# Retiming the start of a fused attention and phase-mixing kernel: another engine for one root, an earlier table load, open theta sums, a last store on two queues

## The chip, the cores and the metric

The kernel runs on one core of one Trainium2 chip. The metric is the device time of one execution in microseconds, as the median of several runs. The core has five engines with an instruction queue each, and each queue is worked off in order: TensorE (PE, with PEld for its weight loads), VectorE (DVE), ScalarE (ACT), GpSimd (POOL) and SyncE (SP, which here issues nearly all DMA transfers). An instruction that waits holds up everything behind it in its own queue.

## The reference, cut to what matters

There are 8 batches of 576 tokens, 8 heads of 64, so 512 channels.

```python
kv  = einsum('bhsd,bhse->bhde', k, v)          # 64x64 for each head
out = einsum('bhsd,bhde->bhse', q, kv)
x   = out / sqrt(mean(out*out) + 1e-6) * g_norm # normed over each head's 64
theta = x @ w_theta
zr, zi = x*cos(theta), x*sin(theta)
y = einsum('ts,bsd->btd', w_tok_r, zr) + einsum('ts,bsd->btd', w_tok_i, zi)
u = x + y
result = u + maximum(u @ w_ch, 0)
```

## The kernel before, in words

A batch is cut into four blocks of 128 tokens and a tail, block 4, of 64 tokens. For each batch, with the line of the main instruction: the loads of q, k and v for the four head pairs (L415, L421); a cast of q to 16 bits (`qcast`, L600; the tail of q, `ql`, L606); turning q on PE (`qTps` L783, copied to `qT` L794/L796); k transposed times v on PE (`kv` L662), copied into a block-diagonal `kvbd` (L816/L818); the product `raw` (L823 by head pair, L699 by block); its square (`sq` L830/L706), the sum over 64 (`ss` L836/L710), one over the root (`rt`), the normed `xp` or `x` (L860/L733); its turn (`xTps` L871/L943, copied to `xT` L882/L884/L952); the phase `th` (L996, block 4 L1001), rounding (`pt` L1008 on ACT, `f` L1012 and `fa` L1019 on DVE), sine and cosine (`tr` L1031, block 4 L1039, on ACT), the product `z` (L1049); the token mix `y` (L1092), `uT` (L1103); the channel product `vps` (L1150), `u` turned back by PE (`ups` L1141, copied on ACT L1157) or by a transposing DMA (`ub`), the sum `ot` (L1161) and the store (L1168, block 4 in two halves L1173).

Batches 0 and 1 go by head pair (`by_pair`, L803), so that work starts when the first pair has landed; the others go by block. The root is taken in two ways. The head pairs of batch 0 and the tail block of batch 0 use ACT's Sqrt (L843, L725) and a reciprocal on DVE (L847, L729). All others use POOL: an addition (L851/L717) and a power of -0.5 (L855/L721). ACT's Sqrt and Sin come from different function tables. Sqrt's is loaded at the start, and the task `sin` (L563) loads Sin's once, after the last Sqrt.

The token-mix weights come by casting DMAs that POOL issues (`wnat`, `wnatl`, L511, L516), are turned on PE (`wTps` L579) and copied to `wT` (L587/L589). `w_theta` comes through a staging tile `wst` in four chunks and is cast to `wth` (L490 on ACT, L492 on DVE). `wch` (L544) is issued by POOL after the load of a given v tile (`WCH_AFTER`, by a small copy to `late`, L385).

The order on every engine is not written by hand. Every piece of work is a task with the engines that may do it, a cost, a due time, and the tasks and buffer slots it needs (`weave.add`). A list scheduler (`Weave.run`) goes through a modelled time and picks by start and due time; `DUE`, `PERIOD`, `START`, `SLOTS` and a few margins are its only knobs. Where PE would be idle the plan puts `warm` matmuls on a constant (L395) that nothing reads. Each engine gets its instructions in the order in which they were picked. Tiles have few buffers: `ql` has one, so that the load of batch 1's `ql` waits for the cast of batch 0's, with every later load behind it on SP's queue.

```python
BANK = {"th": "mm", "y": "mm", "vp": "mm", "pu": "tp", "px": "tp"}
SLOTS: "raw": 2, "tp": 2, "mm": 3, "k": 6, "v": 6, "q": 6, "ql": 1, ...
pu_on = not U_FROM <= b < B - 1 or ti == NF     # u by PE, else by DMA
```

Of the kernel before, what the change touches and what calls it, by code (L numbers as in the profile page):

```python
# [17 lines left out]

PERIOD = 26.95
START = 4.0  # L20
DUE = {
    "load": (-21.61, 8.44),
    "theta": (0.39, 0),
    "mixers": (17.6, 0),
    "wch": (24.7, 1.25),
    "wT": (21.7, 1.67),
    ("phase", 0): (19.67, 0),
    ("mix", 0): (28.68, 4.96),
    ("channel", 0): (31.53, 7.53),
    ("phase", 1): (11.06, 3.64),  # L30
    ("mix", 1): (31.68, 5.24),
    ("channel", 1): (50.99, 7.88),
    ("first", 1): (-24.56, 1.26),
    "first": (0.46, 0),
    "cast": (27.66, 0.92),
    "turn_q": (-15.49, 0.49),
    "attention": (-2.51, 1.53),
    "norm": (-1.15, 4.11),
    "turn": (4.17, 1.73),
    "phase": (18.31, 3.76),  # L40
    "mix": (51.46, 2.87),
    "channel": (75.2, 4.3),
}
# [8 lines left out]
Q_DMA = 4  # L52
U_FROM = 2
X_FROM = 8
MIX_AFTER = 2
WCH_AFTER = 8
KV_RUN = 1
Q_SOFT = 0
QL_SOFT = 1


class Transfers:

    LANES = 8

    def __init__(self):
        self.soft, self.hard, self.done = [], [], {}

    def serve(self, at, left):
        for (a, b) in self.soft:
            if at < a:
                step = min(a - at, left)
                (at, left) = (at + step, left - step)
            if left > 0 and at < b:
                step = min((b - at) / 2, left)
                (at, left) = (at + 2 * step, left - step)
        return at + left
# [4 lines left out]
    def add(self, name, at, took, soft):  # L84
        if soft:
            begin = max(at, self.soft[-1][1] if self.soft else 0.0)
            self.soft.append((begin, begin + 2 * took))
            self.done[name] = begin + 2 * took + 0.3
            free = None
            for (n, arrive, length) in self.hard[-24:]:  # L90
                if self.done[n] > begin + 0.2:
                    if free is None:
                        free = self.before[n]
                    self.before[n] = free
                    free = self.serve(max(arrive, free), length)
                    self.done[n] = free + 0.2
            return
        last = self.done[self.hard[-1][0]] - 0.2 if self.hard else 0.0
        if not self.hard:
            self.before = {}  # L100
        self.before[name] = last
        self.hard.append((name, at, took))
        self.done[name] = self.serve(max(at, last), took) + 0.2


class Weave:
# [7 lines left out]

    SLACK = {"PE": 0.2, "ACT": 0.004, "DVE": 0.078, "POOL": 0.1, "SP": 0.05}
    MARGIN = {"PE": 0.247, "ACT": 0.026, "DVE": 0.555, "POOL": 0.1, "SP": 0.0}
    BEGIN = {"PE": 1.6, "ACT": 3.2, "DVE": 1.7, "POOL": 2.5, "SP": 0.73}
    WARM = 69.7
    COLD = 5.0
    URGENT = 5.5  # L120
    AHEAD = 0.3
    HOLD = 2.45
    DRAIN = 0.095
# [21 lines left out]
    def run(self):  # L145
# [25 lines left out]
        while ready:  # L171
            best = {}
            for t in ready:
# [8 lines left out]
                for (e, cost, lat, port) in engines:  # L182
                    new = e == "PE" and self.ARRAY[port] != form
                    clear = free[e] + self.DRAIN if new else free[e]
                    start = max(clear, at + self.MARGIN[e], port_free if port is True else 0.0)
                    if name[0] == "warm" and start > self.WARM:
                        continue
                    if due < self.URGENT:
                        start = max(clear, start - self.AHEAD)
# [25 lines left out]
            if e == "PE" and not hot:  # L215
                if start > free[e] + 0.4:
                    streak = start
# [45 lines left out]
def kernel(  # L263
# [13 lines left out]
    nc = tc.nc  # L277
# [95 lines left out]
    def sp(cost):  # L373
        return ("SP", cost, cost, False)
# [4 lines left out]
    def soft(took):  # L379
        return (2.4, took, True)  # L380
# [21 lines left out]
    def load(b, hp):  # L402
# [48 lines left out]
        if hp == (0 if b else HP - 1):  # L451
            for (i, (kind, src)) in enumerate((("kl", k), ("vl", v), ("ql", q))):
                if b < QUAD and kind != "ql":
                    continue
                if kind == "ql" and QL_SOFT and b > 1:
                    def fetch(e):
# [4 lines left out]
                              needs=[("qc", b, 0)], uses=[f"qc{b}"], dma=soft(0.9))  # L461
                    continue
                weave.add((kind, b), [sp(0.64)], due("load", b, hp) + (0.04 if b else 1.15) + 0.01 * i,
                          tail(kind, src),
# [5 lines left out]
    def load_weights():  # L470
# [38 lines left out]
        for (i, w) in enumerate((moe_w_tok_r, moe_w_tok_i)):  # L509
# [8 lines left out]
            def part(which, i=i):  # L518
                def fn(e):
# [8 lines left out]
                    else:  # L528
# [5 lines left out]
            weave.add(("wnatl", i), [("POOL", 0.56, 0.56, False)], use + 0.2 + i, rest,  # L534
                      needs=["hold_mix"], dma=soft(0.5))
            weave.add(("wtt", i, 0), [act(P * 2), dve(0.3, True), pool(P * 2)], use + 8, part(0),
# [25 lines left out]
        def table(e):  # L562
            nc.scalar.activation(out=warm[:], in_=pio2_t[:], func=AFT.Sin)  # L563
        weave.add("sin", [("ACT", 1.5, 1.6, False)], due("first", 0, HP + 2), table,
                  needs=[("rt0", hp) for hp in range(HP + 1)] + [("xTp", 0, HP - 1)])

# [124 lines left out]
    def norm(b, ti):  # L691
# [30 lines left out]

        def root0(e):
            t = st[ss]
            nc.scalar.activation(out=t[:], in_=t[:], func=AFT.Sqrt, bias=eps_t[:])  # L725

        def invert0(e):
            r = st[rt] = sb("rt", [P, H], FP32, rt)
            nc.vector.reciprocal(r[:], st[ss][:])  # L729

        def scale(e):
# [27 lines left out]
        weave.add((ss,), [dve(0.59)], at, total, needs=[(sq,)], makes=[("ss", ss)], uses=[sq])  # L759
        if b == 0:  # L760
            weave.add(("rt0", HP), [("ACT", 0.2, 0.35, False)], at, root0, needs=[(ss,)], uses=[ss])
            weave.add((rt,), [dve(0.12)], at, invert0, needs=[("rt0", HP)], makes=[("rt", rt)],
                      uses=[ss])
        else:
            weave.add((rt,), [("POOL", 2.0, 2.1, False)], at, root, needs=[(ss,)], makes=[("rt", rt)],
                      uses=[ss])
        weave.add((x,), [dve(0.6)], at, scale, needs=[(rt,)], makes=[("x", x)], uses=[raw, rt])
# [35 lines left out]
    def by_pair(b, hp):  # L803
# [3 lines left out]
        home = "xT" if b else "uT"  # L807
        bank = "mm" if b == 0 and hp > 1 else "raw"
        (qTn, bdn, kvn, xn, xTn) = (f"{n}{b}" for n in ("qT", "bd", "kv", "xp", "xT"))
# [176 lines left out]
    def phase(b, ti):  # L986
# [58 lines left out]
        def apply(e):  # L1045
# [8 lines left out]
        full = ti < NF  # L1054
        weave.add((th,), [pe(0.866) if full else pe(0.436, "H")], at, product,
                  needs=([("xTp", b, hp) for hp in range(HP)] if b < 2 and full else [("xT", b, ti)])
                  + [("wth", kc) for kc in range(NK)],
                  makes=[(BANK["th"], th)], uses=[f"xT{b}"])
        weave.add((pt,), [act(n, 1)], at, whole, needs=[(th,)], makes=[("pt", pt)], uses=[th])
# [65 lines left out]
    def channel(b, ti):  # L1125
# [39 lines left out]
        def store(e):  # L1165
# [6 lines left out]
            for (half, r) in parts:  # L1172
                nc.sync.dma_start(out=out[b, SF:S, r * n:(r + 1) * n], in_=t[half])  # L1173

# [15 lines left out]
        elif ti == 0:  # L1190
            for kc in range(NK):
# [9 lines left out]
                  makes=[("ot", ot)], uses=[vp, u if pu_on else f"ub{b}"])  # L1201
        weave.add(("out", b, ti), [sp(0.46 if full else 0.9)], at, store, needs=[(ot,)],
                  uses=[ot], dma=dma(0.66 if full else 0.6))
# [64 lines left out]
```

## Time and profile before

| what | value |
|---|---|
| median of 6 runs | 214.2 us (213.51 to 216.27) |
| the profiled execution: time, span | 214.86 us, 213.1 us |
| PE busy | 203.7 us, 96% of the span, 2305 matmuls |
| DVE, ACT, POOL busy | 177.2, 150.3, 89.0 us |
| DMA moved | 45.62 MB, mean 214 GB/s |
| warm matmuls | 50 |
| granted PE clock | 0.99 |

The profile is one execution. The span runs from the first instruction to the last; about 1.8 us of the execution's time lie outside it. A row of the timeline gives the start, the length, the engine, the line and the tile. The length of one matmul or one DVE or ACT instruction contains its run-through time; what an engine needs for one in a row of them is the distance from start to start, which is shorter (0.216 us for a 512-wide matmul, 0.056 us for a 128-wide transpose, 0.60 us for a DVE instruction whose row says 0.69).

### The profile page before, as it was taken

The numbers are of one execution on the slowest core, as the hardware profiler recorded it, in microseconds if no ns is written. First come the engines' busy times: TensorE is split into PE (matmuls) and PEld (weight loads), VectorE is DVE, ScalarE is ACT, GpSimd is POOL, SyncE is SP. The second block draws the span as 40 slices with busy tenths as digits, with TensorE's granted clock in tenths as the row PEclk, the third lists the DMA queues.
The fourth block names the chain that finished last, engine by engine and source line by source line (L and its number), as shares of the span: only waits on it lengthen the run. The fifth ranks groups of instructions, "written<-read, shape, count | busy, mean of one in ns | idle before, by whom it ended". The sixth has DMA issues, their size and how long they took to land.

```text
span 213.1 us, 5833 instructions
## 1 busy us (share of the span) xinstructions
PE 203.7 (96%) x2305; PEld 144.5 (68%) x2305; DVE 177.2 (83%) x355; ACT 150.3 (71%) x294; POOL 89.0 (42%) x104
## 2 busy tenths in 40 slices
PE   6898989999999999999999999999999999999992
PEld 4775567876588777677777577765787467568560
DVE  3297589877978889999999998999999989973652
ACT  2166799967984999898897859789688588550031
POOL 8040106595106663474474436584475733000000
PEclk9996999999999999999999999999999999999999
DMA  6999999998587898978888999759874262334424
GB/s 179 389 365 253 266 366 284 378 236 173 105 273 240 214 287 291 242 261 175 243 175 152 297 345 204 146 142 284 254 166 86 88 174 63 140 109 98 145 104 172
DMA packets 62463, 45.62 MB, mean 214 GB/s; under 512 B 33380, under 2 KB 55524, under 8 KB 62436
## 3 DMA queue, kind: packets, MB, share of 16 engines
q1 hardware_dynamic: 58272, 43.01, 70.0%
q0 software_dynamic: 4160, 2.25, 8.3%
q8 instruction: 18, 0.29, 0.6%
q14 instruction: 9, 0.07, 0.1%
q10 hardware_dynamic: 4, 0.00, 0.0%
HBM read 33.06 MB, written 9.44 MB: 199 GB/s over the span
## 4 chain that ended last, share of the span: by engine, by line
PE 74%; ACT 10%; DMA 6%; DVE 6%; POOL 1%; issue 1%; SPq 1%; DVEq 0%
PE y L1092 29%; PE vps L1150 14%; PE th L996 11%; PE kv L662 7%; DMA wst<-in_moe_w_theta_dram 3%; PE xTps L943 3%; PE raw L699 3%; DMA k<-in_k_dram 2%; ACT tr L1031 2%; PE ups L1141 2%; PE warm L395 2%; PE th L1001 1%; ACT tr L1039 1%; ACT pt L1008 1%; DVE x L733 1%
## 5 line engine op out<-in xcount | busy, mean ns | idle before, releaser
L1092 PE MATMUL y<-wT,z 128*128 128x320 f16 (+1 forms) x576 | 78.1, 286 | 0.1
L1092 PEld LDWEIGHTS <-z 128*128 128x128 f16 x576 | 55.0, 98 | 16.2 <-issue 0.6
L721 POOL TENSOR_TENSOR rt<-ss,mhalf 128x8 f32<-128x8 f32 x31 | 55.8, 1801 | 2.6
L1150 PE MATMUL vps<-wch,uT 128*128 128x512 f16 (+1 forms) x192 | 36.3, 344 | 0.1
L1103 DVE SCALAR_TENSOR_TENSOR uT<-y,gcol,xT 128x320 f16<-128x320 f32 (+1 forms) x48 | 29.2, 610 | 6.9 <-PE y L1092 6.9
L1008 ACT ACTIVATE pt<-th,magic_t 128x512 f32<-128x512 f32 (+1 forms) x40 | 25.8, 645 | 9.2 <-PE th L996 5.8
L996 PE MATMUL th<-wth,xT 128*128 128x512 f16 x128 | 32.0, 379 | 0.0
L717 POOL TENSOR_SCALAR ss<-ss 128x8 f32<-128x8 f32 x31 | 8.4, 272 | 55.7 <-DVE ss L710 54.9
L1012 DVE SCALAR_TENSOR_TENSOR f<-pt,th 128x512 f32<-128x512 f32 (+1 forms) x40 | 25.0, 625 | 2.9 <-ACT pt L1008 2.9
L662 PE MATMUL kv<-v,k 128*64 128x64 f32 (+1 forms) x672 | 26.0, 226 | 0.4 <-DMA v<-in_v_dram 0.4
L662 PEld LDWEIGHTS kv<-v,k 128*64 128x64 f32 (+1 forms) x672 | 23.2, 140 | 4.2 <-issue 3.2
L1031 ACT ACTIVATE tr<-fa,pio_t 128x512 f16<-128x512 f32 x32 | 23.1, 721 | 1.8 <-DVE fa L1019 1.6
L1031 ACT ACTIVATE tr<-f 128x512 f16<-128x512 f32 x32 | 20.2, 631 | 5.5 <-DVE f L1012 5.3
L952 ACT ACTIVATE xT<-xTps,gcol 128x512 f16<-128x512 f16 (+1 forms) x32 | 20.1, 629 | 5.3 <-PE xTps L943 5.1
L710 DVE TENSOR_REDUCE ss<-sq 128x8 f32<-128x512 f32 x32 | 21.7, 678 | 2.2 <-ACT sq L706 2.2
L733 DVE TENSOR_TENSOR x<-raw,rt 128x512 f16<-128x512 f32 x32 | 21.9, 683 | 1.8 <-POOL rt L721 1.3
L1150 PEld LDWEIGHTS <-uT 128*128 128x128 f16 (+1 forms) x192 | 14.7, 102 | 11.4 <-issue 0.6
L1157 ACT COPY u<-ups 128x512 f16<-128x512 f16 (+1 forms) x20 | 9.9, 500 | 16.8 <-PE ups L1141 16.8
L1049 DVE TENSOR_TENSOR z<-x,tr 128x1024 f16<-128x1024 f16 (+1 forms) x32 | 19.6, 615 | 1.5 <-ACT tr L1039 1.2
L706 ACT ACTIVATE sq<-raw 128x512 f32<-128x512 f32 x32 | 19.0, 593 | 0.5 <-PE raw L699 0.5
L996 PEld LDWEIGHTS <-xT 128*128 128x128 f16 x128 | 11.5, 98 | 10.1 <-ACT xT L952 0.2
L600 DVE CAST qcast<-q 128x512 f16<-128x512 f32 x32 | 13.2, 420 | 5.3 <-DMA q<-in_q_dram 5.3
(105 smaller groups left out, 265.7 us busy)
## 6 DMA issues: line engine op xcount, KB each, us to landing
q<-in_q_dram SPq DMA_DIRECT2D x32, 256.0 KB, 4.9
out_dram<-ot SPq DMA_DIRECT2D x32, 256.0 KB, 3.0
k<-in_k_dram SPq DMA_DIRECT2D x24, 256.0 KB, 5.0
v<-in_v_dram SPq DMA_DIRECT2D x24, 256.0 KB, 4.9
k<-in_k_dram SPq DMA_DIRECT2D x8, 288.0 KB, 5.6
v<-in_v_dram SPq DMA_DIRECT2D x8, 288.0 KB, 5.4
wst<-in_moe_w_theta_dram SPq DMA_DIRECT2D x4, 256.0 KB, 7.4
out_dram<-ot SPq DMA_DIRECT2D x16, 64.0 KB, 2.1
```

The costliest lines, as they stand in the source:

```text
L662: nc.tensor.matmul(kvp[r * D:(r + 1) * D, hp, :], kt, vt, start=(j == 0), stop=(j == (NT if b >= QUAD else NS) - 1),)
L710: nc.vector.reduce_sum(out=t[:], in_=st[sq][:].rearrange("p (h e) -> p h e", h=H), axis=mybir.AxisListType.X,)
L721: nc.gpsimd.tensor_tensor(out=r[:], in0=t[:], in1=mhalf[:], op=ALU.pow)
L733: nc.vector.tensor_tensor(out=t[:].rearrange("p (h e) -> p h e", h=H), in0=st[raw][:].rearrange("p (h e) -> p h e", h=H), in1=st[rt][:].un ...
L952: nc.scalar.activation(out=st["xT", b][:, :, cols], in_=st[px][:, :, 0:cols.stop - cols.start], func=AFT.Copy, scale=gcol[:],)
L996: nc.tensor.matmul(t[:], xT[:, kc, :], wth[:, kc, :], start=(kc == 0), stop=(kc == NK - 1),)
L1008: nc.scalar.activation(out=t[:], in_=st[th][:], func=AFT.Identity, bias=magic_t[:])
L1012: nc.vector.scalar_tensor_tensor(out=t[:], in0=st[pt][:], scalar=MAGIC, in1=st[th][:], op0=ALU.subtract, op1=ALU.subtract,)
L1031: nc.scalar.activation(out=t[:, which, :], in_=src[:], func=AFT.Sin, scale=-RAD, bias=0.0 if bias is None else bias[:],)
L1092: nc.tensor.matmul(st[y][:, c, :], z[:, kc * P:(kc + 1) * P], wT[m][:, cols], start=(c == 0 and m == 0) if open_sums else m == 0, stop=m = ...
L1103: nc.vector.scalar_tensor_tensor(out=st["uT", b][:, chunks, cols], in0=st[y][:], scalar=gcol[:], in1=st["xT", b][:, chunks, cols], op0=ALU ...
L1150: nc.tensor.matmul(t[half], uT(kc), wch[:, kc, r * n:(r + 1) * n], start=(kc == 0), stop=(kc == NK - 1),)
```

## The change

Seven things are changed in the code.

1. The root of batch 0's tail block goes by POOL, as in all other batches; L725 and L729 are gone.
2. The task `sin` no longer waits for the tail block's Sqrt nor for `xTps` of pair 3; it waits for the four head pairs' Sqrt only.
3. For blocks 0 and 1 of batch 0 (`TH_OPEN = 2`) the theta sum is two tasks: three of the four channel chunks, which need head pairs 0 to 2, and then the last chunk. The sums stay open in their banks in between. The head pairs' `raw` of batch 0 keep to the two `raw` banks, where pairs 2 and 3 had used `mm`.
4. The last store's two halves go by two queues, SP's and ACT's.
5. `U_FROM` goes from 2 to 3: batch 2's u is turned by PE (16 transposes, 4 copies on ACT) and no longer by four transposing DMAs.
6. `WCH_AFTER` goes from 8 to 7: the load of `wch` is held for the last v of batch 1 and not for the first of batch 2.
7. The scheduler's knobs change: due times, period, margins, and the share that it gives to POOL's transfers. `KL_SOFT = 0` adds a branch that is not taken.

```diff
-PERIOD = 26.95
+PERIOD = 26.64
...
-U_FROM = 2
+U_FROM = 3
...
-WCH_AFTER = 8
+WCH_AFTER = 7
+TH_OPEN = 2
+KL_SOFT = 0
...
-        weave.add("sin", [("ACT", 1.5, 1.6, False)], due("first", 0, HP + 2), table,
-                  needs=[("rt0", hp) for hp in range(HP + 1)] + [("xTp", 0, HP - 1)])
+        weave.add("sin", [("ACT", 1.5, 1.6, False)], due("first", 0, HP), table,
+                  needs=[("rt0", hp) for hp in range(HP)])
...
-        if b == 0:
-            weave.add(("rt0", HP), [("ACT", 0.2, 0.35, False)], at, root0, needs=[(ss,)], uses=[ss])
-            weave.add((rt,), [dve(0.12)], at, invert0, needs=[("rt0", HP)], makes=[("rt", rt)],
-                      uses=[ss])
-        else:
-            weave.add((rt,), [("POOL", 2.0, 2.1, False)], at, root, needs=[(ss,)], makes=[("rt", rt)],
-                      uses=[ss])
+        weave.add((rt,), [("POOL", 2.0, 2.1, False)], at, root, needs=[(ss,)], makes=[("rt", rt)],
+                  uses=[ss])
...
-        bank = "mm" if b == 0 and hp > 1 else "raw"
+        bank = "mm" if b == 0 and hp > 1 and not TH_OPEN else "raw"
...
+        if b == 0 and ti < TH_OPEN:
...
+            weave.add((th, "a"), [pe(0.65)], at - 2.0, sums(range(NK - 1)),
+                      needs=[("xTp", b, hp) for hp in range(HP - 1)] + [("wth", kc) for kc in range(NK - 1)],
+                      makes=[(BANK["th"], th)], uses=[f"xT{b}"])
+            weave.add((th,), [pe(0.217)], at, sums([NK - 1]),
+                      needs=[(th, "a"), ("xTp", b, HP - 1), ("wth", NK - 1)], uses=[f"xT{b}", th])
...
-                nc.sync.dma_start(out=out[b, SF:S, r * n:(r + 1) * n], in_=t[half])
+                queue = nc.scalar if b == B - 1 and r else nc.sync
+                queue.dma_start(out=out[b, SF:S, r * n:(r + 1) * n], in_=t[half])
```

What the scheduler makes of it, read from the order of the two built programs:

- PE, before: `xTps` of pair 2, fillers, `xTps` of pair 3, fillers, theta of blocks 0 to 3, then the first `wTps`. After: `xTps` of pairs 2 and 3, `wTps0`, theta of blocks 0 and 1 over three chunks, `wTps1`, `wTps2`, the last chunk of both, theta of block 2, `wTps3`, theta of block 3.
- ACT, after, from the last head pair's Sqrt on: the Sin table, a copy of `wnatl0`, `wT0`, the cast of `wst_3`, `wT1`, `pt` of blocks 0 and 1, `wT3`, sine and cosine of blocks 0 and 1, then the turned tail of q.
- POOL, after: casts `wst_0`, copies from `wnat0`, casts `wst_2`; before it did neither cast nor the copy.
- DVE: the cast of batch 0's `ql` stood ahead of the first `f` and stands behind `fa` of block 1 now.
- PE work ahead of the first matmul of `y` chunk 2 of batch 0 (`y0_2`) is the same set of matmuls in both programs, but for 49 fillers before and 54 after. Behind it the sets differ by batch 2's 16 transposes and one filler, and their order differs in places.

## The prediction

> **What bounds the kernel now.** I read the sums by stage first, then PE's waits, then ACT's and SP's timelines over the first 45 us, then the landing times. The sums by stage (start:end, length, busy time of PE, PEld, DVE, ACT, POOL with instructions, granted clock, DMA share, GB/s):
>
> ```profile
> 0.00:21.45 21.45, 17.79 (x232) 13.01 (x233) 11.67 (x34) 9.22 (x23) 7.62 (x20) 0.92 0.95 296
> 21.45:44.40 22.95, 21.70 (x324) 16.39 (x322) 17.61 (x40) 20.45 (x44) 8.95 (x11) 1.00 1.07 326
> 44.40:64.60 20.20, 20.20 (x267) 14.09 (x265) 17.55 (x35) 16.35 (x32) 7.17 (x9) 1.00 0.92 188
> ...
> 95.50:155.30 59.80, 59.80 (x688) 42.93 (x687) 58.10 (x114) 48.75 (x92) 32.70 (x33) 1.00 0.89 221
> ```
>
> From 44.40 on PE has no idle time: that is where `y0_2`, the third chunk of batch 0's mix, begins (timeline: 44.38). DVE is nearly as full from 95 to 155. PE's waits from 44.4 to 208 confirm it (one line in all):
>
> ```profile
> PE xTps L943 <- DVE x L733: 0.2, 1, 0.2
> ```
>
> So everything behind 44.38 is PE work, and the end moves with (a) the moment at which PE reaches `y0_2`, (b) PE work added behind it, (c) new waits there, (d) the tail. Ahead of `y0_2` PE has slack (50 fillers, mostly there), and ACT is the full engine: 20.45 of 22.95 us. Its timeline there, with the table load in the middle:
>
> ```profile
> 15.13 0.63 ACT L490 ACTIVATE wth<-wst 128x512 f16<-128x512 f32 x1 [1.09 <-DMA wst<-in_moe_w_theta_dram]
> 15.66 0.41 ACT L816 CAST kvbd<-kv 64x64 f16<-64x64 f32 x2
> ...
> 22.51 0.69 ACT L1008 ACTIVATE pt<-th,magic_t 128x512 f32<-128x512 f32 x1 [1.84 <-PE th L996]
> ...
> 27.26 0.31 ACT L725 ACTIVATE ss<-ss,eps_t 128x8 f32<-128x8 f32 x1
> 27.59 1.28 ACT L563 ACT_TABLE_LOAD   x1
> 28.88 0.20 ACT L563 ACTIVATE warm<-pio_t 128x1 f32<-128x1 f32 x1
> 29.11 0.47 ACT L952 ACTIVATE xT<-xTps,gcol 128x256 f16<-128x256 f32 x1
> 29.48 0.62 ACT L1031 ACTIVATE tr<-f 128x512 f16<-128x512 f32 x1
> ...
> 41.11 1.03 ACT L1039 ACTIVATE tr<-fa,pio_t 64x256 f16<-64x256 f32 x2
> ```
>
> The first sine starts 7.0 us after the first `pt`, the last cosine ends at 42.14, and `y0_2` starts 2.2 us later. SP's timeline shows a hole in the loads:
>
> ```profile
> 12.84 0.92 SPq L421 DMA_DIRECT2D v<-in_v_dram  x1
> 21.39 0.63 SPq L434 DMA_DIRECT2D ql<-in_q_dram  x1
> ```
>
> It waits for the cast of batch 0's `ql` (20.95), the one buffer of that tile.
>
> **The change part by part: the way to `y0_2`.** I follow the new order with the row lengths of before; on one engine from start to start, across engines by the whole row.
>
> *Head pairs to theta.* Before, pair 3's `kvbd` copies stood behind the cast of `wst_0` (15.13 to 15.66), and from there to the end of pair 3's `xT` (DVE, 20.55 + 0.48 = 21.03) it took 5.4 us. Now POOL has that cast: the copies go at 14.55, behind `kv` of pair 3 (13.38 + 1.15). DVE takes two turns more in between, and `xT` ends near 19.9: 1.1 us earlier.
>
> *A new wait eats it.* `wTps0` now stands ahead of theta on PE. The tile view of `wnat` gives 9.0 us from issue (11.24) to landing, so 20.24; `wnatl` 8.9 us from 12.03, so 20.9. Behind it wait the open sums. They also need the cast of `wst_2`, on POOL behind its copy of `wnat0` (20.25 + 0.40). No row shows a POOL cast of 128x512; the memset of 64x512 took 0.52, twice the 128x256 copy is 0.8, twice that for its two operations is 1.6. I take 0.8, as the copy is the nearest kind: 21.5. Then six 512-wide matmuls (0.216 each, from start to start) 1.3, `wTps1` and `wTps2` 0.56, a filler 0.1, the last chunk 0.2 and 0.2 of run-through: `pt` of block 0 starts at 23.65, against 22.51. The open sums thus gain nothing: theta is 1.1 us later.
>
> *PE is empty from about 19.4 to 21.0,* but for a filler. The longest idle time of PE before, behind its start, is 0.6 us (0.64 at 17.58), and the granted clock is 1.00 after 21.45, so no row prices a longer one: nothing as the lower end, and as the upper a second cold phase like the first `kv` pair (1.85 us against 1.26 later), 0.6 us for each 1.3 us of work, some 1.7 in all. I take nothing, as these gaps are nearer to 0.6 than to the 1.5 us of idle start. The Trainium skill ("TensorE: Matmul & The Clock Gate", Part 1) has the gate close after an idle window of some 3.4 us; by that rule it costs nothing too, and only a landing 2 us later would change that.
>
> *The table load.* It leaves the full stretch of ACT (1.28 + 0.20) for the idle one near 18 to 19.5, with the tail's Sqrt (0.31). The first sine now waits only for `f`, `pt` of block 1 and `wT3`: about 25.5 against 29.48, and `z` of block 0 starts at 27.75 against 32.22. The Trainium skill ("ScalarE: Activation LUTs", What ACT_TABLE_LOAD costs) adds 1.38 us of drain to such a load; here the next instruction starts 1.29 us after it, so the row decides; by the page the gain on ACT would be 1.4 larger.
>
> *ACT's queue.* From `pt` of block 0 to the last cosine of block 4 the new order has, from start to start, 2.3 of `pt`, 0.7 of block 4's short `pt` and `xT`, 4.5 of sine and cosine, 1.9 of block 4's, 2.0 of squares, 0.5 of `wT`, 2.9 of `qT`, 1.3 of `kvbd`: 16.1 us, so 39.75 at the earliest. Waits come on top where latency binds: `qT` of pair 1 (0.4), `xT` of block 4 behind `kv` and `x0_4` (0.8), `kvbd` of pair 2 (0.4), block 4's sine and cosine behind `f`, `fa` (0.7): 42.05. Then `z` (0.35), its hops and the last four matmuls: `y0_2` at 43.0. Gain 1.4 us. Ends: 3.0 with no wait on ACT, since PE's own work (some 18 us from 23.4, its changes of weight shape counted) sets 41.4 then; 0 if the latencies add 1.4 more.
>
> *The tail's root by POOL.* `ss` at 30.7, then 0.3 to 1.3 (L851: 0.23 to 1.28) and 1.7: 32.8 to 33.9. DVE is at `z` of block 2 until 34.2 then; that covers it. Without the cover the cost is up to 1.
>
> *SP's hole grows.* The cast of `ql` now stands on DVE behind `fa` of block 1, near 26.7, so `ql` of batch 1 is issued 5.3 us later, and behind it `q`, `k`, `v` of pairs 1 to 3 and all of batch 2. Before, `ql` took 5.2 us because the queue still held loads until 26.1 (`v` at 12.84 landed after 13.3). Now it finds the queue empty: 2.75 us like the first load, 29.5; the rest follow 0.67 us apart as before: `v` of pairs 1, 2, 3 at 31.5, 33.5, 35.5. PE wants them at about 33, 36, 39, DVE wants `ql` at 31.0. Cost nothing; with 5.2 us for `ql`, 0.6 on DVE's queue and so on the chain.
>
> **Behind `y0_2`.** Batch 2's 16 transposes: four groups of 0.22 (`ups` at 55.02, next at 55.24): +0.9. Its four copies (0.50 each) lie on ACT, which has 11 us free of 59.8 in 95.5:155.3. The transposing DMAs go, and nothing waited for them. Changes of weight shape behind `y0_2` are 52 in both programs: 0, give or take 0.2. DVE takes five `qT` copies of 0.34 more and one of 0.28 less between 44 and 72 (+1.4); it has 2.65 us free in 44.40:64.60 alone. Price 0, and if that cover is gone 1.4. `wch` is issued by POOL near 37.2 and 38.0 instead of 44.92; a landing takes 7.2 to 7.7, so 45.7; `vps` of blocks 0 and 1, now ahead of `y0_4`, wants it at 46.1. Cost nothing, but see the rivals.
>
> **The tail.**
>
> ```profile
> 209.12 0.33 SPq L1168 DMA_DIRECT2D out_dram<-ot  x1
> 209.61 1.12 SPq L1173 DMA_DIRECT2D out_dram<-ot  x2
> ```
>
> The second half is issued 0.53 after the first (210.14) and takes 2.0 to land. On ACT's queue it is issued with the first: -0.55 (an issue on ACT took 0.38 at the start, so no more is lost). The tail block of batch 6 moves from ahead of `y7_0` to behind `y7_5`; same work, 0.
>
> **Sum:** -1.4 + 0.9 - 0.55 = -1.05 us. The profiled run took 214.86 with a span of 213.1, 0.66 above the median of 214.2; so a span of 212.05, a run of 213.8, and against the median **213.2 us**.
>
> **Rivals.**
>
> 1. *ACT runs without waits.* For it: the 16.1 us, and that ACT ran with under 1 us of idle time from 22.5 to 42.1 before. Against it: the chain of latencies above. `y0_2` at 41.4: -3.0 + 0.9 - 0.55, so 211.5. Chance 0.23.
> 2. *The way to `y0_2` is no shorter.* Theta starts 1.1 later, and POOL's cast or `ql` takes its upper price. `y0_2` at 44.4: 214.5. Chance 0.17.
> 3. *`wch` lands late; slower.* POOL's transfers took 7.2 to 11.9 us before (`wnat` 11.9), and now the two are issued while SP catches up its 5 us. PE waits in order at `vps` of block 0, with all of its later work behind it. A landing 8.1 us after the second issue at 38.0 is the point from which it costs; 11.9 costs 3.8: 217.0. Slower by over 1% from 11.2 on. For it: `qcast` issued at 41.82 into a full queue took 7.3 for a quarter of the bytes. Against it: both `wch` of before, also into a full queue, 7.2 and 7.7. Chance 0.12.
>
> **How the numbers follow.** My forecast (212.3 to 214.3 of its own) has 0.48. A run of six spread by over 1%, so 1% is about what can be told from no change: faster means under 212.06, slower over 216.34. Rival 1 (0.23) lies under 212.06 for the most, and a little of the forecast does: 0.26. Rival 3's upper part and unnamed new waits of PE over 3 us: 0.12. The rest is 0.62. The range for 8 in 10 reaches down to rival 1 and up to rival 3's middle: 211.2 to 215.9.
>
> **What would show it.** The Sin table load near 18 to 19.5 in ACT's timeline; PE idle before `wTps`, ended by `wnat`; `pt` first at 23.65; a first sine near 25.5; SP's `ql` near 26.7; `y0_2` at 43.0; no wait of PE for `wch`; PE without idle time behind; two issues side by side at the end. Wrong would be: `pt` before 22.5, PE waits of over 1 us behind `y0_2`, or `v` of batch 1 as what ends them.

## The result and the profile after

The changed kernel takes 216.39 us (median of 17 runs, 214.95 to 219.61), the kernel before 214.49 (38 runs, 213.30 to 217.29). The ratio is 1.0084, 95% interval 1.0058 to 1.0111: some 1.8 us slower, where 213.2 had been forecast. The profiled execution took 218.61 us with a span of 216.8; it is one of the long executions that the ratio leaves out.

The sums by stage of the changed kernel, in the columns of the prediction's first view:

```profile
0.00:21.45 21.45, 16.44 (x245) 12.69 (x246) 11.14 (x32) 9.35 (x23) 9.24 (x23) 1.00 0.96 294
21.45:44.40 22.95, 21.28 (x302) 15.86 (x301) 16.82 (x38) 18.45 (x39) 10.04 (x14) 0.93 0.76 211
44.40:64.60 20.20, 18.68 (x219) 12.90 (x220) 17.47 (x37) 13.29 (x25) 7.20 (x8) 1.00 1.13 286
```

ACT has been relieved: 18.45 us of 22.95 between 21.45 and 44.40, where it had 20.45. But PE is busy for only 18.68 of the 20.20 us behind 44.40, where it had no idle time at all, and the DMA share has moved: 0.76 in the second stage (1.07 before), 1.13 in the third (0.92 before). PE's waits of the whole run name the stretch:

```profile
PE vps L1174 <- DMA wch<-in_moe_w_ch_dram: 1.5, 1, 1.5
...
PE wTps L598 <- DMA wnat<-in_moe_w_tok_r_dram: 1.1, 1, 1.1
PE kv L681 <- DMA v<-in_v_dram: 0.9, 1, 0.9
...
PE wTps L598 <- DMA wnatl<-in_moe_w_tok_r_dram: 0.8, 1, 0.8
...
PE th L1002 <- ACT xT L958: 0.6, 1, 0.6
```

Two of these lie behind `y0_2`: the first and the last. PE's timeline shows the large one in the middle of `vps` of block 0: two chunks of the channel mixer's weight are there, the other two are not, and as PE works in order everything stands behind them.

```profile
48.62 0.60 PE L1174 MATMUL vps<-wch,uT 128*128 128x512 f16 x2
50.75 0.59 PE L1174 MATMUL vps<-wch,uT 128*128 128x512 f16 x2 [1.52 <-DMA wch<-in_moe_w_ch_dram]
```

In the trace the two transfers are issued by POOL at 39.98 and 40.79 and land at 48.58 and 50.70, 9.9 us for the second. Behind them stands SP's timeline, with the hole that the prediction had seen:

```profile
12.48 0.99 SPq L426 DMA_DIRECT2D v<-in_v_dram  x1
28.42 0.62 SPq L439 DMA_DIRECT2D ql<-in_q_dram  x1
29.09 0.62 SPq L420 DMA_DIRECT2D q<-in_q_dram  x1
```

Sixteen microseconds without a load (8.5 before), then three pairs of batch 1 and batch 2's loads at once, with `wch` among them. ACT's timeline shows what the change was made for:

```profile
17.18 1.28 ACT L582 ACT_TABLE_LOAD   x1
...
25.39 1.27 ACT L1014 ACTIVATE pt<-th,magic_t 128x512 f32<-128x512 f32 x2 [0.54 <-PE th L1067]
...
27.41 1.15 ACT L1037 ACTIVATE tr<-f 128x512 f16<-128x512 f32 x2
```

The table load sits in ACT's free stretch and the first sine starts at 27.41 instead of 29.48, although `pt` starts at 25.39 instead of 22.51. Yet `y0_2` starts at 45.48 in the trace, against 44.38. Each execution also has its mean granted clock; it is 0.992 here, and 0.990 in the profile of before.

### The profile page after: what moved, and what is told of

It is laid out like the page before. It is cut to its first block, busy times and chain, and to the rows that moved or that the text cites. A ratio compares the mean times of both kernels' runs of the same rounds, so it can differ in the third digit from the quotient of the medians.

```text
span 216.8 us, 5888 instructions
## 1 busy us (share of the span) xinstructions
PE 203.8 (94%) x2325; PEld 145.3 (67%) x2325; DVE 177.8 (82%) x357; ACT 148.5 (68%) x290; POOL 92.1 (42%) x110
## 4 chain that ended last, share of the span: by engine, by line
PE 74%; DMA 15%; ACT 4%; DVE 2%; SPq 2%; issue 1%; POOL 1%; DVEq 0%; POOLq 0%
PE y L1116 28%; PE vps L1174 13%; PE th L1002 12%; PE kv L681 7%; DMA v<-in_v_dram 6%; DMA wch<-in_moe_w_ch_dram 5%; DMA wnatl<-in_moe_w_tok_r_dram 4%; PE raw L718 3%; PE xTps L949 3%; PE ups L1165 2%; PE th L1007 2%; ACT tr L1037 1%; PE th L1067 1%; SPq L426 1%; ACT tr L1045 1%
## 5 line engine op out<-in xcount | busy, mean ns | idle before, releaser
L1174 PE MATMUL vps<-wch,uT 128*128 128x512 f16 (+1 forms) x192 | 37.0, 344 | 1.5 <-DMA wch<-in_moe_w_ch_dram 1.5
L736 POOL TENSOR_SCALAR ss<-ss 128x8 f32<-128x8 f32 x32 | 10.2, 318 | 60.7 <-DVE ss L729 59.7
L1002 PE MATMUL th<-wth,xT 128*128 128x512 f16 x120 | 29.7, 379 | 0.6 <-ACT xT L958 0.6
L681 PE MATMUL kv<-v,k 128*64 128x64 f32 (+1 forms) x672 | 25.2, 222 | 0.9 <-DMA v<-in_v_dram 0.9
L681 PEld LDWEIGHTS kv<-v,k 128*64 128x64 f32 (+1 forms) x672 | 22.5, 136 | 4.3 <-issue 2.3
L1181 ACT COPY u<-ups 128x512 f16<-128x512 f16 (+1 forms) x24 | 12.2, 514 | 17.9 <-PE ups L1165 17.9
L729 DVE TENSOR_REDUCE ss<-sq 128x8 f32<-128x512 f32 x32 | 21.7, 677 | 2.3 <-ACT sq L725 2.2
L1174 PEld LDWEIGHTS <-uT 128*128 128x128 f16 (+1 forms) x192 | 14.5, 102 | 12.1 <-issue 2.6
L725 ACT ACTIVATE sq<-raw 128x512 f32<-128x512 f32 x32 | 19.0, 593 | 1.6 <-PE raw L718 1.5
L1002 PEld LDWEIGHTS <-xT 128*128 128x128 f16 x120 | 10.9, 98 | 11.1 <-ACT xT L958 1.3
```

The source lines that it names most:

```text
L681: nc.tensor.matmul(kvp[r * D:(r + 1) * D, hp, :], kt, vt, start=(j == 0), stop=(j == (NT if b >= QUAD else NS) - 1),)
L729: nc.vector.reduce_sum(out=t[:], in_=st[sq][:].rearrange("p (h e) -> p h e", h=H), axis=mybir.AxisListType.X,)
L1002: nc.tensor.matmul(t[:], xT[:, kc, :], wth[:, kc, :], start=(kc == 0), stop=(kc == NK - 1),)
L1174: nc.tensor.matmul(t[half], uT(kc), wch[:, kc, r * n:(r + 1) * n], start=(kc == 0), stop=(kc == NK - 1),)
```

## The experiments

Unless another base is named, a kernel is the changed one with a small edit that leaves the order on every queue as it was. Ratios are to the kernel before, on the same chip.

**Fillers where PE waits for `wnat`.**

```diff
-            nc.tensor.matmul(... warm ...)
+            for _ in range(22 if n == 44 else 1):
+                nc.tensor.matmul(... warm ...)
```

> The changed kernel, with the filler ahead of the first mixer transposes (warm44) issued 22 times and not once; no other instruction moves. Theory A (PE was empty for 1.9 of the 2.3 us before 21.3, so its clock was granted at half from 22.4 to 25.5: theta of blocks 0 and 1 took 0.427 us a matmul): the clock stays full, pt of block 0 starts near 23.8 and not at 25.39, y0_2 1.0 to 1.6 us earlier, ratio to the kernel before near 1.002. Rival B (the landing of the mixer weights and ACT's queue set the way to y0_2, the clock is beside the point): y0_2 within 0.3 us of 45.48, ratio unchanged near 1.008.

Measured: 218.28 us, ratio 1.0182 (1.0132 to 1.0232). The clock was 1.00 throughout the head, but PE's timeline shows that the fillers were too many:

```profile
21.51 2.56 PE L401 MATMUL warm<-kvbd 128*128 128x256 f16 x22
23.91 0.39 PE L599 MATMUL wTps<-ident,wnat 128*128 128x128 f16 x4
```

`wnatl` landed at 21.84, and `pt` of block 0 started 4.84 us behind that, where it starts 2.68 us behind it in seven of the eight other profiles of this order at full clock: the fillers cost 2.2 us there. By the ratios the time is 2.1 us above that of the changed kernel, give or take 1.2, so a delay ahead of theta reaches the end, in full as far as these numbers go. None of the six executions had a mean clock of 0.992 or less; that bears on theory A and is counted with the eight fillers below. The `wch` wait of 1.5 us stayed. (Behind the first chunk of `w_theta`, this profile's loads were issued 1.3 to 2.3 us later than in the profile of after, so the two are not compared by their absolute times.)

**A buffer of its own for each `ql`: SP's hole taken away.**

```diff
-                t = sb("ql", [T, H, D], FP32, f"ql{b}")
+                t = work.tile([T, H, D], FP32, tag=f"ql{b}", bufs=1, name=f"ql{b}")
```

> The changed kernel with a buffer of its own for each of the two ql tiles; the order of every queue is the same. Theory A (the hole of SP's queue from 13.5 to 28.4 makes batch 1's loads late, and with them wch, which is held for the last v of batch 1): ql of batch 1 is issued near 13.5, v of pair 3 of batch 1 lands before 34 and not at 39.8, the wait of 1.5 us for wch shrinks to under 0.5, ratio near 1.002. Rival B (my prediction's view that the hole costs nothing and wch is late for its own transfer alone): loads earlier, wch still waited for by over 1 us, ratio near 1.008. A third outcome, that earlier loads push back the landing of the mixer weights, would show as wnat landing after 21 and a ratio above 1.01.

Measured: 214.98 us, ratio 1.0019 (0.9988 to 1.0050): 1.4 us regained (1.0084 - 1.0019 of 214.4). SP issues `ql` of batch 1 right behind the loads of batch 1's first head pair, and the next `v` a little earlier than before the change (22.18, 23.52 then):

```profile
12.85 0.33 SPq L426 DMA_DIRECT2D v<-in_v_dram  x1
13.57 0.96 SPq L439 DMA_DIRECT2D ql<-in_q_dram  x1
...
22.18 0.43 SPq L426 DMA_DIRECT2D v<-in_v_dram  x1
```

`wch` is issued at 37.52 and 38.33 and takes 6.8 and 8.1 us; `vps` of block 0 runs through, and from 44.4 to 208 PE waits once:

```profile
PE th L1002 <- ACT xT L958: 0.6, 1, 0.6
```

**`wch` issued early, the hole left.**

```diff
                 nc.gpsimd.dma_start(out=wnatl[i][0:T], in_=w[SF:S, :])
+                for h in range(2 * i):
+                    nc.gpsimd.dma_start(out=wch[:, 2 * h:2 * h + 2, :], in_=moe_w_ch[...])
```

> The changed kernel with both transfers of wch issued right behind the last mixer transfer (near 14) and no longer at 40; everything else stands where it did. Theory A (PE's wait at vps of block 0 is paid in full, since PE works in order and has no slack behind y0_2): the wait goes, 1.5 us less, ratio near 1.001. Rival B (what PE loses there it would lose later, to DVE or ACT): the wait goes, the time falls by less than 0.5 us, ratio over 1.006.

The two issues at their old place are left out. Measured: 215.21 us, ratio 1.0026 (0.9994 to 1.0058). `ql` is still issued at 26.85 and `kv` of batch 1 still waits 0.2 us for `v`, but the `wch` wait is gone. Two repairs with nothing in common but the time at which `wch` is there regain the same 1.2 to 1.4 us: the wait for `wch` is the main loss, and without SP's hole it does not arise. The hole costs a little ahead of `y0_2` too: from `pt` of block 0 to `y0_2` it is 19.99 us here and 20.06 in the one-queue kernel, against 19.75 with the `ql` buffers.

**The last store on one queue again.**

```diff
-                queue = nc.scalar if b == B - 1 and r else nc.sync
+                queue = nc.sync
```

> The changed kernel with the last store's two halves both on SP's queue, as before the change. Theory A (prediction: the second issue comes 0.53 us later and the end moves with it): 0.5 us slower than the changed kernel, ratio near 1.011. Rival B (in the profile of the changed kernel the span ends 3.4 us after the two issues and in that of before 3.5 us after the first of its two, so ACT's queue ends no earlier): no difference, ratio near 1.008.

Measured: 218.75 us, ratio 1.0139, but only from 1.0070 to 1.0208 (six runs, most of them at a lower clock), so the time settles nothing. The span ends 4.32 us behind the last product, against 4.01 in the changed kernel.

**Fillers taken from the kernel before.**

```diff
+            if 20 <= n <= 36:
+                return
             nc.tensor.matmul(... warm ...)
```

> The kernel before the change, with the fillers 20 to 36 of TensorE left out (it multiplies constants there between 16.5 and 21.5 us; nothing reads them), so that TensorE has empty stretches there like those of the changed kernel. Theory A (an empty stretch of some 1 to 2 us in the head makes the clock drop, as in the profiled run of the changed kernel, where it was at half speed from 22.4 to 25.5): the first rows of theta of block 0 show a granted clock of 0.5 and a pitch of 427 ns instead of 216, the first z comes up to 1.6 us later, the kernel is 0.5 to 0.8% slower than before. Theory B (the drop belongs to that one execution, and the empty stretch is free): the pitch stays at 216 ns, the time is within 0.2% of before.

Measured: 216.01 us, ratio 1.0062 (1.0029 to 1.0095). The sums by stage, granted clock third from the end:

```profile
16.00:18.00 2.00, 1.01 (x14) 0.59 (x12) 1.86 (x5) 1.56 (x5) 0.00 (x0) 1.00 1.08 249
18.00:20.00 2.00, 0.32 (x4) 0.14 (x4) 1.80 (x4) 1.47 (x4) 0.00 (x0) 1.00 1.08 260
20.00:22.00 2.00, 1.79 (x9) 0.82 (x10) 0.96 (x3) 0.47 (x2) 0.00 (x0) 0.73 1.05 252
22.00:24.00 2.00, 2.00 (x6) 0.76 (x5) 1.11 (x2) 1.11 (x3) 0.00 (x0) 0.50 1.08 234
```

PE is almost empty from 18.3 to 20.2, and then the clock is halved, from 20.9 to 24.3: theta's matmuls follow each other after 427 ns instead of 216. All 12 executions had a mean clock of 0.992 or less. Theory A holds, in that an emptied PE makes the clock drop. From the first `pt` to `y0_2` it takes 23.12 us, 1.2 more than in the two profiles of the kernel before's head that follow (21.88 and 21.87). The size in the time is mixed, as `wch` happened to land late here too (a wait of 1.0 us in the profile).

**The kernel before with the last store on two queues.**

```diff
-                nc.sync.dma_start(out=out[b, SF:S, r * n:(r + 1) * n], in_=t[half])
+                queue = nc.scalar if b == B - 1 and r else nc.sync
+                queue.dma_start(out=out[b, SF:S, r * n:(r + 1) * n], in_=t[half])
```

> The kernel before the change with nothing altered but the last store: its second half is issued by ACT instead of SP, as in the changed kernel. The prediction's term: 0.55 us less behind the last product, so about 213.9 us, ratio 0.9975. What the pair of the changed kernel with and without this part shows (4.0 us from the last product to the end of the span against 4.3): 0.3 us, ratio 0.9985. A rival, that the end is set by the landing of the store and not by its issue: 0, ratio 1.000. The span minus the end of the last product (4.12 in the profile of before) tells these apart better than the time: 3.6, 3.8 or 4.1.

Measured: 214.18 us, ratio 0.9996 (0.9963 to 1.0029); the end of the span lies 3.84 us behind the last product, 0.28 less than before. More telling is its head, which is that of the kernel before, instruction by instruction. First its sums by stage, then those of the profile that the prediction was made from:

```profile
16.00:18.00 2.00, 1.61 (x13) 0.85 (x12) 1.69 (x4) 1.76 (x5) 0.00 (x0) 1.00 1.06 233
18.00:20.00 2.00, 1.63 (x16) 1.15 (x15) 1.47 (x5) 0.54 (x2) 0.00 (x0) 1.00 1.08 264
```

```profile
16.00:18.00 2.00, 1.18 (x12) 0.70 (x12) 1.47 (x4) 1.95 (x5) 0.00 (x0) 0.97 1.05 237
18.00:20.00 2.00, 2.00 (x12) 1.07 (x11) 1.57 (x4) 0.93 (x3) 0.00 (x0) 0.50 1.11 273
20.00:22.00 2.00, 2.00 (x14) 1.44 (x13) 0.81 (x2) 0.40 (x1) 0.00 (x0) 0.68 1.05 249
```

The profiled execution of before had a clock drop of its own, from 17.9 to 21.3; its mean clock is 0.990. In the two-queue kernel pair 3's `xT` ends at 19.96 instead of 21.03, `pt` starts at 21.33 instead of 22.51, and `y0_2` at 43.21 instead of 44.38. Most of that is not the clock. ACT's timeline here has no wait ahead of the cast of `wst_0`, where before it waited 1.09 us for the landing:

```profile
13.88 0.62 ACT L490 ACTIVATE wth<-wst 128x512 f16<-128x512 f32 x1
14.64 0.42 ACT L816 CAST kvbd<-kv 64x64 f16<-64x64 f32 x2
```

The first chunk of `w_theta` landed at 13.28 here and at 15.11 before, and pair 3's `kvbd` copies stand at 14.64 against 15.66: 1.0 of the 1.2 us is there before the clock drops. From these copies to the end of `xT` it takes 5.37 us in the profile of before and 5.31 to 5.33 in every other one. What the drop can have cost lies between there and `pt`: 0.1 us against this execution, at most 0.5 against the shortest such stretch at full clock (1.04 us, in the ninth experiment; 1.48 before).

**Both repairs** (the edits of the `ql` buffers and of the early `wch`).

> The changed kernel with both repairs of its transfers: a buffer of its own for each last q tile, and the two transfers of the channel mixer's weight issued behind those of the token mixer's. If the late weight was the whole loss and either repair alone removes it: as with either alone, 214.9 to 215.2 us, ratio 1.002 (0.999 to 1.005), with the third block of y of batch 0 near 43.4. If each repair also takes a different wait away (with the early weight alone a wait of 0.2 for v and one of 0.4 behind the transposes of q stayed): 214.5 us, ratio 1.000. If the two crowd the transfers between 14 and 28 us: the loads of the head land later, ratio above 1.004.

Measured: 214.66 us, ratio 1.0001 (0.9978 to 1.0024), the best of the changed family, and level with the kernel before. `y0_2` starts at 43.04, 19.71 us behind the first `pt`; in the kernel before that is 21.9.

**PE work added behind the head** (base: a buffer for each `ql`).

```diff
+            for _ in range(2 if b < 3 and ti < NF else 1):
                 (the transposes of a full block)
```

> The changed kernel with a buffer of its own for each last q tile (so that the channel mixer's weight comes in time), in which every full block of batches 0 to 2 is transposed by TensorE twice, the second time over the first: 48 transposes more, at the pitch of some 55 ns of those there 2.6 us of TensorE. If TensorE is the bound behind the head, as the term of 0.9 us for the 16 transposes that batch 2 has taken on says, the time grows by 2.6 us over the same kernel without them, ratio to before 1.014 (1.010 to 1.018). If TensorE has slack there and those 16 cost little, the ratio is under 1.006.

Measured: 216.91 us, ratio 1.0109 (1.0063 to 1.0154), so 1.9 us above the same kernel without them (214.98), against 2.6 for a PE that is never idle. That is 0.6 us for 16 transposes, give or take 0.4 by the two intervals: they are not free, and whether they cost all of PE's time for them (0.9) is not settled.

**Root and Sin table alone, on the kernel before.** The diff's parts on `root0`, `invert0`, `rt` and `sin`, nothing else.

> The kernel before the change with one part of it alone: the root of batch 0's tail by POOL, the Sin table loaded behind the head pairs' Sqrt, the planner's settings as they were (it works out the whole order anew). Theory A (the table load and the Sqrt in ACT's full stretch set the way to the third block of y of batch 0, as the prediction had it): the first sine near 25.5 instead of 28 to 29.5, the third block of y 1 to 1.5 us earlier than the 43.2 of the undisturbed head, the time 0.4 to 0.7% below before. Theory B (the way to it is as long as PE's and DVE's own work and the waits between engines make it, and an earlier sine only waits elsewhere): the third block of y within 0.5 us of 43.2, ratio 0.998 to 1.003.

Measured: 219.49 us, ratio 1.0233 (1.0193 to 1.0274). ACT's timeline has the sine earlier than in any other kernel:

```profile
22.04 0.69 ACT L995 ACTIVATE pt<-th,magic_t 128x512 f32<-128x512 f32 x1 [1.16 <-PE th L983]
...
23.49 0.62 ACT L1018 ACTIVATE tr<-f 128x512 f16<-128x512 f32 x1
```

First sine at 23.49 instead of 28.32 (two-queue kernel), first product of `y` at 31.79 instead of 33.25, and yet `y0_2` at 44.80 instead of 43.21. The head of this execution also began later (pair 3's `kvbd` copies at 15.69 against 14.64), but counted from these copies `y0_2` still comes 0.5 us later and not 1 us earlier. The last cosine of block 4, which was to set the way, ends at 36.95, 7.9 us ahead of `y0_2`. Theory A is refuted in this order. Its size can't be put down to this part, since the planner orders all 214 us anew; 3.7 of the 5 us arise behind `y0_2`.

**Eight fillers, both repairs.** As the first experiment, with 8 for 22.

> The changed kernel with both repairs of its transfers, and the filler ahead of the transposes of the token mixer's weight issued 8 times instead of once (0.9 us of TensorE in the place where it waits for that weight; 22 times, 2.4 us, made it late). Theory A (empty TensorE there makes the clock drop in some executions): none of the executions has a mean granted clock of 0.992 or less, where 6 of 18 of the changed kernel and 2 of 12 with both repairs had one; those at full clock take 214.5 us as without the fillers, ratio 1.000. Theory B (the drop is not set off by the empty stretch): the share of executions at 0.992 or less stays at one in six or more. If 0.9 us of fillers already delays the weight: 0.3 to 0.5 us more than without.

Measured: 215.11 us, ratio 1.0032 (1.0008 to 1.0057). None of 12 executions was at a mean clock of 0.992 or less. In the profile PE worked 0.79 us of the 2.00 between 20 and 22, and the clock stayed:

```profile
20.00:22.00 2.00, 0.79 (x9) 0.39 (x7) 0.00 (x0) 0.22 (x1) 0.98 (x2) 1.00 1.02 238
22.00:24.00 2.00, 2.00 (x19) 1.30 (x18) 0.00 (x0) 1.36 (x4) 0.00 (x0) 1.00 1.09 227
```

With fillers in this place (here, in the first experiment and in the last) none of 24 executions was at 0.992 or less, against 19 of 72 of the changed order without them: the fillers keep the clock. They gain nothing at the median. The time is 0.7 us above that with both repairs, give or take 0.7; in the trace the fillers end at 20.27, ahead of the landing of `wnat` at 20.44, so they delay nothing there.

**Batch 2 turned by DMA again, both repairs; and with the eight fillers.**

```diff
-U_FROM = 3
+U_FROM = 2
```

> The changed kernel with both repairs of its transfers, and with the full blocks of batch 2 turned by DMA again as before the change (U_FROM 2; the order is the same up to batch 2's channel mixing and worked out anew behind it). If TensorE is the bound there: 16 transposes of 55 ns less, 0.9 us, so 213.6 us, ratio 0.996. If the transfers that come back take it away (the queue of SP holds loads and stores behind each of them): ratio 0.999 to 1.003.

> All four repairs in one: a buffer of its own for each last q tile, the early transfers of the channel mixer's weight, 8 fillers ahead of the token mixer's transposes, and batch 2 turned by DMA. If the loss is made up of the late weight, the clock in some executions and the 16 transposes: 213.6 us, ratio 0.996 (0.993 to 0.999), no execution at a mean clock of 0.992 or less. If the head has no gain to give and the rest only cancels: ratio 0.999 to 1.002.

Measured: 216.11 us, ratio 1.0084 (1.0053 to 1.0116), and 216.69, ratio 1.0137 (1.0094 to 1.0179). PE's waits from 44.4 to 208 of the first:

```profile
PE th L1004 <- ACT xT L960: 1.5, 2, 0.9
PE xTps L951 <- DVE x L746: 0.7, 1, 0.7
```

Sixteen transposes fewer, and 1.6 us of waits more than the 0.6 of the kernel with both repairs. One reading is that PE's transposes had covered these latencies; that is not shown. Whether DMA's side or only the new order costs it is open.

The open theta sums and the scheduler's knobs were not run alone, so what each of them gives or takes is not known.

## Why the prediction was wrong

*The step that decided: "Cost nothing" for `wch`, and for SP's hole ahead of it.* The hole came as forecast: `ql` issued at 27.16 in the one-queue kernel (26.7 forecast) and landed 2.82 us later (2.75). What failed is the next sentence, that the rest would "follow 0.67 us apart as before". Their issues did, 0.53 us apart, but with three pairs and batch 2's loads in the queues together `v` of pairs 1 to 3 landed at 33.26, 36.44 and 38.49 (31.5, 33.5, 35.5 forecast). POOL's issue of `wch`, held for `v`, slipped from 38.0 to 39.49 there and 40.79 in the profile of after, and its second landing took 9.8 and 9.9 us where I had written 7.7. That is the third rival, whose point of 8.1 us was passed: 1.5 us of waiting, 1.2 to 1.4 us of time by each repair. The rival had the mechanism and the sign; I gave it 0.12 since both transfers of before "also into a full queue" took 7.2 and 7.7. Over the nine traces in which it was issued between 36 and 47 us the second takes from 7.7 to 9.9 us, so one execution's figure was no bound. Against the kernel with `ql` buffers the second landing of the one-queue kernel is 2.8 us later: 1.2 by the issue and 1.7 by the length. The first of these is the hole's; the length is 8.9 and 9.8 also in two traces of the kernel before's order, with the shorter hole, so how much of it the hole makes is open.

*The reference of the head.* The walk itself was good. At full clock, `pt` of block 0 starts at 23.33 with both repairs and 23.59 with the `ql` buffers (23.65 forecast, though the terms as written add up to 23.86), the first sine at 25.22 and 25.48 (25.5), the last cosine of block 4 ends at 42.08 and 42.39 (42.05), `y0_2` starts at 43.04 and 43.34 (43.0). The new wait sets it: `pt` starts 2.68 us behind the landing of `wnatl` in seven of the eight profiles of this order at full clock, the first experiment's aside (2.95 in the other), and moves with it from 22.79 to 24.44. But the walk was set against the head of one execution, and heads differ by 1 us between executions. Against its 44.38 the gain is 1.3; against the 43.21 of the two-queue kernel it is 0.2. That execution is the early one of four: pair 3's `kvbd` copies stand at 14.64 in it, at 15.66, 15.69 and 15.81 in the other three profiles with the old order up to there. So the gain of a typical execution lies between, and no run here fixes it closer. ACT's timelines, of the two-queue kernel and of the one with both repairs, give the last cosine:

```profile
39.95 1.02 ACT L1039 ACTIVATE tr<-fa,pio_t 64x256 f16<-64x256 f32 x2
```

```profile
41.05 1.03 ACT L1047 ACTIVATE tr<-fa,pio_t 64x256 f16<-64x256 f32 x2 [0.45 <-DVE fa L1027]
```

Against this execution it comes 1.1 us later with the change, in spite of a sine that comes 3.1 us earlier (25.22 against 28.32): theta starts 2.0 us later, because `wTps0` waits, and latencies of DVE stand on the way. Against it the second rival was right; against the profile of before the forecast was. *Pair 3's `xT` 1.1 us earlier* rested on ACT's wait for `wst` ahead of the copies, which the two-queue kernel's profile does not have: there the old order ends that `xT` at 19.96, and the changed order's profiles have 19.4 to 20.9 (22.2 in the first experiment's).

*The last line of the sum.* It took 0.66 off because the profiled run lay above the median, and also a gain measured against that same run's head. As far as the head is what made the run long, that is the same time twice. From the walk, 213.8 was the forecast to make.

*PE empty: "I take nothing".* In the profile of after the drop is there, from 22.1 to 25.5, and `pt` starts 4.22 us behind the landing of `wnatl`, where the same order at full clock has 2.68: 1.5 us, near the upper end of 1.7. It comes in some executions: a mean clock of 0.992 or less in 6 of 18 of the changed kernel and 2 of 12 with both repairs, in 2 of 69 of the kernel before, timed beside the experiments. The 6 have a median of 218.5 us, the other 12 one of 216.3. So the upper end was the better figure, in one execution of three. The Trainium skill ("TensorE: Matmul & The Clock Gate", Part 1) has the gate close after an idle window of some 3.4 us, and such windows run on freely, whatever the kernel does. I compared 3.4 us with single gaps, and passed over the 0.92 of the first stage, which was a drop already. The traces agree on the length (the last section) but not on idleness: PE had worked 1.53 of the 3.41 us ahead of the drop in the profile of after, and 2.07 in that of before, and the measurement decides.

*The tail, -0.55.* The mechanism is right and the size was off: 0.28 on the kernel before, 0.3 between the changed kernel and its one-queue form. In the profile of after the two issues start together:

```profile
213.41 0.47 SPq L1198 DMA_DIRECT2D out_dram<-ot  x1
213.41 0.55 ACTq L1198 DMA_DIRECT2D out_dram<-ot  x1
```

But the span ends 3.4 us after them, where before it ended 2.95 after the second issue. The changed family ends 0.2 us later behind its last product on either number of queues (4.32 against 4.12 on one, 4.01 against 3.84 on two), and not so with `U_FROM` 2 (3.82); why is open.

*Batch 2's 16 transposes, +0.9*: 0.6, give or take 0.4, by doubling. *New waits behind `y0_2`*: one of 0.58 us at 93.85 (0.59 at 90.0 with the `ql` buffers), `th` for ACT's `xT`, where before had 0.23 at 94.92; the forecast had none. *POOL's root of the tail* cost nothing, as forecast (1.68 us, ended at 32.7 with both repairs, and DVE was at `z` until 33.1), and POOL's cast of `wst_2` took 0.61 to 0.62 (0.8 taken).

Together: from `y0_2` to the last product the kernel with both repairs takes 165.64 us, against 164.92 in the two-queue kernel and 164.59 in the profile of before; its tail is 0.1 shorter than the old one. With -0.2 or -1.3 on the way to `y0_2`, by which execution is taken, that is +0.4 or -0.4, and by its time the kernel is level with before, within 0.5 us. The late `wch` adds 1.2 to 1.8 (by one repair, and by both), and the clock some 2 us more in a third of the executions.

## What to carry to other kernels

Before a gain is read off one profile, look in the very stretch that is to be shortened at its granted clock and at its waits for landings, and find the same stretch in other executions: here one landing 1.8 us later made a head 1.0 us longer, and the wait for it was on show. When a change holds a queue back, add up all the bytes that it will then move at once, and price each other queue's landing in that stretch with the range over several executions; a weight that is wanted once, in order, by the engine that has no slack should be issued before such a stretch, not in it. An engine relieved on the critical way need not give anything by itself: follow the latest input of the step that counts, here the landing of `wnatl`.

## What the runs showed of the hardware

The granted clock of PE fell to half for 3.41 us each time: 17.88 to 21.29 (profile of before), 22.07 to 25.48 (after), 20.91 to 24.32 (fillers taken), read from sums over half microseconds. No idle stretch of that length stood ahead: PE had worked 2.07, 1.53 and 1.10 us of the 3.41 before the drop. A mean clock of 0.992 over a span of some 215 us is one such phase (half of 3.41 is 0.8% of it). With eight fillers PE worked 1.9 us in the emptiest 3.4 us of the head and the clock stayed; whether that is the amount of work or where the 3.4 us began is not settled here.

The same two POOL transfers of `wch` took 6.8 to 8.8 us (the first) and 7.7 to 9.9 (the second) in the nine traces in which they were issued between 36 and 47 us, and 12.5 to 14.5 where they were issued near 14 among the loads of the head. An issue on a second queue at the end saved 0.3 us of the 0.53 that lay between the two issues. The first of the four loads of `wst` (256 KB each), issued between 7.3 and 8.3 us in all fourteen traces, took 5.6 to 7.4 us to land.
